# Four uneven zero transfers behind the last pass over wq, and twelve zero pieces sent as halves: a two-layer decode backward kernel on one core

## The chip, the core and the metric

The kernel runs on one core of one Trainium2 chip. The core has a matmul engine (PE, with its weight loads shown as PEld), a vector engine (DVE), a scalar engine (ACT), a general engine (POOL) and a queue engine (SP). Sixteen DMA engines move data between the chip's memory and the core's on-chip buffer (SBUF, 128 partitions). The metric is device time of one execution in microseconds, the median of several runs; less is better.

## The reference, cut to what matters

One token goes through two rounds of the same attention block A and the same MLP block B, and the kernel returns the output and all gradients.

```
def _fwd_reference(A_x, A_k_cache, A_v_cache, A_wq, A_wo, B_x, B_w1, B_b1, B_w2):
    x = A_x
    x = x + _A_ref(_layernorm(x), k_cache, v_cache, wq, wo)   # attention on the last 4096 of 32768 cache rows
    x = x + _B_ref(_layernorm(x), w1, b1, w2)                 # h * tanh(softplus(h)) MLP
    x = x + _A_ref(...)                                        # the same weights again
    x = x + _B_ref(...)
    return x
_out, _vjp = jax.vjp(_f, A_x, A_k_cache, A_v_cache, A_wq, A_wo, B_w1, B_b1, B_w2)
return (_out, *_vjp(grad_out))
```

Shapes: D = 1024, 32 query heads in 4 groups, head size 128, MLP width 3584, all bf16. The two cache gradients, `out_2` and `out_3`, are [1, 4, 32768, 128]. Attention reads only the last 4096 rows of each group, so the first 28,672 rows (ZR in the code) of each of the eight group planes are zero: 8 planes of 7 MB, 56 MB of zeros to be written. The rest of the outputs are weight gradients (outer products of two rows, one a round) and the small vectors.

## The kernel before, in words

The forward part streams the weights once or twice through a ring of eight 1 MB slots in SBUF (`ring_t`, class `Ring`; its loads are issued by SP at L71 as a slot comes free), then the backward part streams them again: for round 1 the pass over W1 that lies on the chip (`dn_b1`, L852), then `attn_bwd` (L905) with its pass over wo, the attention products against V and K, and its pass over wq; then round 0 in the same order (L1160 for w2, `dn_b0` L891, `attn_bwd` again). Chunks are transposed on PE, evicted by ACT or DVE, and used as the weights of matrix-vector products.

After the last pass over wq (the end of L1227) a late stage begins: all PSUM becomes four wide tiles, and `work` (L1140) takes turns among generators that make outer products (`unit_dw` L1072, `units_kv` L1122), evict them into 1 MB stages and hand them to SP to be stored (`store`, L1044, issued at L1050 and L1055, in halves or in wholes).

The zeros go beside all this from POOL's own queue. `zt` is a 128 x 4096 tile of zeros, filled by a memset at L811. `zjobs` (L246) is a list of 56 pieces: each of the 8 planes is cut into seven pieces of 128 partitions x 8 KB, 1 MB each. Half of one piece is written early, from another tile of zeros, by SP (L288); its other half, 0.5 MB, is put at the far end of the list (L291), so that it goes last of all. `zeros(n, after)` (L257) takes the next n pieces and issues one transfer for each (L265). With `after`, POOL first copies one element of that tile (L260), so that the transfers behind it on POOL's in-order queue wait for the tile. The number of pieces at each call is written out by hand:

- 1 and 7 around the forward attention of round 1, 8 after it (L841);
- 8 at L997, ahead of `dn_b1`, and 4 at L1001 behind it;
- 4 in `dp3` and 3 in `dq3` (around the round-1 attention products), 1 at L1154, 2 in the pass over w2, 2 at L1174;
- 2 in `do1` at c == 5, 4 in `dp1` and 4 in `dq1` (around the round-0 attention products), 2 in `dn1` at t == 3;
- 4 at L1228, behind the last pass over wq, the 0.5 MB piece last.

POOL also carries small copies: in `do1` at c == 1, `take_back` (L832) brings rows back from scratch memory as five transfers (28 pieces of 256 bytes into one partition, twice; then 2x32, 2x8 and 2x8 pieces into two partitions); at c == 5 and c == 6, `rows_go` (L1038, issued at L1041) moves 8 rows into one partition four times and 7 rows twice. SP's `twins` (L1066, issued at L1070) copy those rows once more for the outer products. In `attn_bwd`, POOL fills the second half of DOC (L927).

Of the kernel before, what the change touches and what calls it, by code (L numbers as in the profile page):

```python
# [15 lines left out]
P = 128  # L16
HQ = 32
DH = 128
# [3 lines left out]
G = 4  # L22
# [71 lines left out]
def kernel(  # L94
# [22 lines left out]
    nc = tc.nc  # L117
# [3 lines left out]
    ZR = Sk - W  # L121
# [9 lines left out]
    def sb(shape, dtype, name):  # L131
        return keep.tile(shape, dtype, name=name)
# [24 lines left out]
    ZC = 4096  # L157
    zt = sb([P, ZC], BF16, "zt")
# [36 lines left out]
    for hi in range(4):  # L195
        r = slice(32 * hi, 32 * hi + 32)
# [49 lines left out]
    zjobs = []  # L246
    for out_t in (out_2, out_3):
        for g in range(G):
            dst = out_t[0, g, 0:ZR, :].rearrange("(p r) d -> p (r d)", p=P).rearrange("p (r c) -> p r c", c=ZC)
            for k in range(dst.shape[1]):  # L250
                zjobs.append(dst[:, k, :])
    zjobs.reverse()

    pz = sb([1, 16], FP32, "pz")
    pz_n = [0]

    def zeros(n, after=None):  # L257

        if after is not None and zjobs:
            nc.gpsimd.tensor_copy(pz[0:1, pz_n[0] % 16:pz_n[0] % 16 + 1], after[0:1, 0:1])  # L260
            pz_n[0] += 1
        for _ in range(n):
            if zjobs:
                dst = zjobs.pop()
                nc.gpsimd.dma_start(dst, zt[:, 0:dst.shape[1]])  # L265


    KEEP_Q = (5, 6, 7)
# [96 lines left out]
    def to_eight(bank, buf):  # L365

        nc.vector.transpose(buf[:, 0:256], bank[:, 0:256])
        return buf[:, 0:256].rearrange("p (g m) -> p g m", m=32)[:, :, 0]
# [434 lines left out]
    def last_da(k):  # L803

        for c in (5, 6):
            if k == 0:
                da_dots(c)
            else:
                ring.release(("2", 0, c))
        if k:  # L810
            nc.gpsimd.memset(zt[:], 0.0)  # L811
            zeros(1)

    def wo_hook1(c):
        if c == 0:
            zeros(7, OC[:, 0, 1:2])
        if c:
            conv(1)
# [4 lines left out]
    def put_by(name, cols, n):  # L823

        b = big().bitcast(BF16)
        nc.tensor.transpose(b[0:2 * n, 0:P], cols[:].rearrange("p n l -> p (n l)"), ident_bf[:])
        r = stg[0:2 * n, len(DR), :]
        nc.scalar.copy(r, b[0:2 * n, 0:P])
        DR[name] = dram.tile([2 * n, P], BF16, name=f"dr_{name}")
        nc.sync.dma_start(DR[name][:], r)  # L830

    def take_back(name, base, off, step=2):  # L832
        r = DR[name][:].rearrange("(n l) p -> l n p", l=2)
        to = ROWS[base:base + 2, off:off + r.shape[1] * P].rearrange("l (n p) -> l n p", p=P)
        for l in range(0, 2, step):
            nc.gpsimd.dma_start(to[l:l + step], r[l:l + step])

    x3, st3, sA1 = attn_fwd(1, x2, st2, False, wo_hook1, last_da)
    put_by("OC", OC, HQ)
    put_by("NA", NA, TD)  # L840
    zeros(8, x3)  # L841
    sB1 = mlp_fwd(1, x3, st3, lambda: conv(1, "A"))
    put_by("NB", NB, TD)
# [4 lines left out]
    dh1, dh0 = mp1, mp0  # L848
# [3 lines left out]
    def dn_b1(g):  # L852

        bcast(lambda c: DHC[:, c, 1:2], STAY)
        mv_open()
        even()
        for t in range(TD):
            rowdot(W1[:, t, 0:STAY * P], [LB[0][:, 0:512]], 512, dnp[:, t:t + 1], True)
            for k in range(3):
                f0, n = STAY + 8 * k, 8  # L860
                w = W1[:, t, f0 * P:(f0 + n) * P]
                turned(w, n, lambda w=w, f0=f0, n=n, t=t, k=k: mv(w, n, TP[:, t:t + 1], lambda i: DHC[:, f0 + i, 1:2], k == 2),
                       None, f_block)
        flush()
        conv(3, "A")
        return ln_bwd(dnp, sB1["n32"], sB1["rstd"], g, "B1", lambda k: conv(k, "A"))
# [3 lines left out]
    def rowize_f():  # L870

        b = big().bitcast(BF16)
        for l in range(2):
            for k in range(4):
                nc.tensor.transpose(b[0:7, (4 * l + k) * P:(4 * l + k + 1) * P],
                                    DHC[:, :, l].rearrange("p (c k) -> p k c", k=4)[:, k], ident_bf[:])
        nc.scalar.copy(rf.rearrange("c (l p k) -> c l p k", l=2, k=4), b[0:7].rearrange("c (l k p) -> c l p k", l=2, k=4))
        for l in range(2):
            rows_out.append((ROWS[64 + l:65 + l, NOFF:NOFF + F].rearrange("o (c j) -> o c j", j=512),
                             rf[:, 512 * l:512 * l + 512]))  # L880
# [113 lines left out]

    nc.vector.tensor_tensor(out=dh1[:], in0=da1[:, 0:TF], in1=mp1[:], op=ALU.mult)
    nc.vector.tensor_copy(DHC[:, :, 1], dh1[:])
    zeros(8, dh1)  # L997
    g3 = dn_b1(g4)
    sB1["act_late"]()
    put_by("AC", AC, TF)  # L1000
    zeros(4, g3)  # L1001

    def dp3():
        zeros(4)
# [22 lines left out]
    def rowize(cols, n, base, off):  # L1027

        b = big().bitcast(BF16)
        nc.tensor.transpose(b[0:2 * n, 0:P], cols[:].rearrange("p n l -> p (n l)"), ident_bf[:])  # L1030
        k = rt_n[0]
        rt_n[0] += 1
        nc.scalar.copy(rt[0:2 * n, k, :], b[0:2 * n, 0:P])
        for l in range(2):
            rows_out.append((ROWS[base + l:base + l + 1, off:off + n * P].rearrange("o (t p) -> o t p", p=P),
                             rt[l:2 * n:2, k, :]))

    def rows_go(queue):  # L1038

        while rows_out:  # L1040
            queue.dma_start(*rows_out.pop(0))  # L1041
# [24 lines left out]
    def twins(*of):  # L1066
        for base, n in of:
            for l in range(2):
                to, of = (base ^ 32) + l, base + l
                nc.sync.dma_start(*(x.rearrange("l (a b) -> l a b", a=16) for x in (TWIN[to:to + 1, 0:n], ROWS[of:of + 1, 0:n])))  # L1070
# [116 lines left out]
    def do1(c):  # L1187
        if c == 1:
            take_back("AC", 96, NOFF, 1)
            take_back("OC", 32, NOFF)  # L1190
            take_back("NB", 64, 0)
            take_back("NA", 0, 0)
        if c == 4:
            y = to_eight(YR, RT.rearrange("p a t s -> p (a t s)")[:, 0:512].bitcast(FP32))
            nc.vector.tensor_tensor(out=x4[:], in0=y, in1=x3[:], op=ALU.add)
        if c == 5:
            rowize(GA, TD, 32, 0)
            rowize(GB, TD, 96, 0)
            rows_go(nc.gpsimd)
            zeros(2)  # L1200
        if c == 6:
            rowize_f()
            rows_go(nc.gpsimd)

    def dp1():
        zeros(4)
        twins((96, NOFF + F), (32, NOFF + J), (64, NOFF + F))
        stage_free.extendleft(VS[:, g].rearrange("p t d -> p (t d)") for g in range(G))

# [7 lines left out]
    def dn1(t):  # L1217
# [6 lines left out]
        if t == 5:  # L1224
            todo[0].append(units_cols(0, 8, out_4))

    g0_rest = attn_bwd(0, sA0, g1, ("o", 3), ("q", 3), (), dict(do=do1, dp=dp1, dq=dq1, dn=dn1))  # L1227
    zeros(4)  # L1228
    stage_free.extendleft(ring_t[:, i, :] for i in range(8))
    stage_free.extendleft(lent)  # L1230

# [50 lines left out]
```

## Time and profile before

| What | us |
|---|---|
| median of 3 runs (lowest, highest) | 450.59 (450.19, 450.88) |
| the profiled execution | 450.31 |
| its span, first to last instruction | 448.5 |
| PE busy | 314.8 (70%) |
| DVE busy | 262.2 (58%) |
| ACT busy | 209.4 (47%) |
| POOL busy | 44.5 (10%) |
| bytes moved by the DMA engines | 181.40 MB, mean 404 GB/s |
| share of POOL's queue (software_dynamic) | 58.26 MB, 31.5% of the 16 engines' span |
| zero transfers, issue to landing, median | 20.7 |

The profile is one execution taken by the hardware profiler. Its page cuts the span into 40 slices of 11.2 us and shows each engine's busy share as a digit. For the DMA engines it gives the mean share of all 16, and what they moved. The windows view gives the same for any stretch of time, and a share can come out a little over 1, since packets overlap at their ends. A wait names who ended it. The trace also has a record for every DMA packet (queue, start, duration, size, but not which of the 16 engines carried it) and the time of every completion step: a transfer completes in 16 steps, one from each DMA engine.

### The profile page before, as it was taken

What the parts mean: (1) busy time and instruction counts of PE and PEld (TensorE: products, weight loads), DVE (VectorE), ACT (ScalarE), POOL (GpSimd) and SP (SyncE); (2) the same over time, 40 slices, a digit from 0 to 9 for tenths busy, and PEclk for the clock granted to TensorE, in tenths of its full rate; (3) what the DMA queues carried; (4) which work ended last, traced back from release to release, by engine and by line L of the source; (5) the groups of instructions that cost most, each with busy time, mean ns of one, the idle gap of its engine ahead of it and who ended that gap; (6) DMA issues with size and microseconds to landing.
All of it is one profiled execution on the core that took longest, in us unless ns stands there. A gap on an engine that the chain in (4) does not pass through costs nothing.

```text
span 448.5 us, 12849 instructions
## 1 busy us (share of the span) xinstructions
PE 314.8 (70%) x5681; PEld 243.3 (54%) x5681; DVE 262.2 (58%) x516; ACT 209.4 (47%) x238; POOL 44.5 (10%) x94
## 2 busy tenths in 40 slices
PE   3835542565698797987987666798877888899600
PEld 3735532445685696986986545798862222234300
DVE  4504746368551664864477447654478998998600
ACT  2501101011058576861474341561348999999700
POOL 1000000001232212102101003023220000000000
PEclk9955555556559799986799657957685555555555
DMA  8999999999999999999999999999999899999994
GB/s 336 422 420 420 419 419 418 418 355 425 400 422 421 422 422 416 397 422 422 424 422 422 427 423 419 405 410 388 405 397 412 347 411 416 416 420 411 409 406 192
DMA packets 30057, 181.40 MB, mean 404 GB/s; under 512 B 3954, under 2 KB 5162, under 8 KB 12082
## 3 DMA queue, kind: packets, MB, share of 16 engines
q1 hardware_dynamic: 21478, 122.30, 66.6%
q0 software_dynamic: 8432, 58.26, 31.5%
q8 instruction: 44, 0.72, 0.6%
q14 instruction: 11, 0.09, 0.0%
q10 hardware_dynamic: 92, 0.02, 0.0%
HBM read 81.84 MB, written 98.62 MB: 402 GB/s over the span
## 4 chain that ended last, share of the span: by engine, by line
DMA 40%; PE 31%; DVE 13%; ACT 5%; issue 4%; SPq 0%; ACTq 0%; DVEq 0%
DMA ring<-in_B_w_dram 13%; PE BIG L489 10%; DMA W<-in_A_wo_dram 9%; DMA ring<-in_A_wq_dram 7%; DMA ring<-in_A_wo_dram 5%; DMA W<-in_B_w_dram 4%; PE TP L508 4%; PE wide L1129 4%; ACT ring L316 3%; PE wide L1078 3%; DVE ring L313 3%; DMA W<-in_A_k_cache_dram 2%; DVE W L313 2%; PE BIG L667 2%; PE MV L956 2%
## 5 line engine op out<-in xcount | busy, mean ns | idle before, releaser
L316 ACT COPY ring<-BIG 128x1024 bf16<-128x1024 bf16 x52 | 51.4, 1014 | 50.0 <-PE BIG L489 30.2
L1078 PE MATMUL wide<-W 2*128 2x512 bf16 x240 | 53.1, 597 | 9.7 <-ACT ring L316 2.4
L489 PE MATMUL BIG<-ident_bf,ring 128*128 128x128 bf16 x672 | 54.5, 234 | 2.0 <-issue 1.2
L489 PEld LDWEIGHTS <-ring 128*128 128x128 bf16 x768 | 51.6, 107 | 3.4 <-issue 2.7
L466 DVE CUSTOM_DVE_ANT_0 junk<-ring,SC 128x1024 bf16<-128x1024 bf16 x32 | 38.9, 1215 | 11.0 <-DMA ring<-in_B_w_dram 10.6
L1078 PEld LDWEIGHTS <-W 2*128 2x128 bf16 x240 | 12.8, 102 | 46.3 <-issue 45.4
L508 PEld LDWEIGHTS <-ring 128*128 128x128 bf16 x864 | 29.9, 98 | 11.7 <-issue 6.3
L316 ACT CAST ring<-wide 128x1024 bf16<-128x1024 f32 (+1 forms) x37 | 34.5, 1015 | 1.1 <-PE wide L1078 1.1
L265 POOL DMA_DIRECT2D out_dram<-zt x56 | 29.9, 538 | 48.8 <-DMA out_dram<-zt 47.9
L313 DVE CAST ring<-wide 128x1024 bf16<-128x1024 f32 (+1 forms) x27 | 31.3, 1198 | 2.8 <-PE wide L1078 2.7
L316 ACT COPY KT<-BIG 128x1024 bf16<-128x1024 bf16 x22 | 21.6, 1007 | 21.8 <-PE BIG L667 19.9
L313 DVE COPY ring<-BIG 128x1024 bf16<-128x1024 bf16 x32 | 21.8, 689 | 15.1 <-PE BIG L489 12.5
L466 DVE CUSTOM_DVE_ANT_0 junk<-ring,DSX 128x1024 bf16<-128x1024 bf16 x24 | 29.4, 1224 | 0.8
L489 PE MATMUL BIG<-ident_bf,W 128*128 128x128 bf16 x280 | 26.9, 255 | 3.1 <-DMA W<-in_A_wo_dram 2.7
L316 ACT COPY W<-BIG 128x1024 bf16<-128x1024 bf16 x20 | 20.1, 1014 | 11.8 <-PE BIG L489 11.6
L551 PE MATMUL MV<-NA,ring 128*128 128x1 bf16 x512 | 15.3, 165 | 13.4 <-DMA ring<-in_A_wq_dram 12.1
L489 PEld LDWEIGHTS <-W 128*128 128x128 bf16 x288 | 21.6, 123 | 3.5 <-DMA W<-in_A_wo_dram 2.9
L551 PEld LDWEIGHTS <-ring 128*128 128x128 bf16 x512 | 14.7, 104 | 14.2 <-DMA ring<-in_A_wq_dram 12.8
L1129 PE MATMUL wide<-W 32*128 32x256 bf16 x128 | 19.7, 403 | 1.5 <-DVE KT L313 0.9
L316 ACT CAST KT<-wide 128x1024 bf16<-128x1024 f32 x19 | 19.1, 1030 | 1.6 <-PE wide L1129 1.1
L316 ACT CAST W<-wide 128x1024 bf16<-128x1024 f32 x16 | 16.0, 1024 | 6.6 <-PE wide L1078 6.2
L354 PE MATMUL YR<-ring,AC 128*32 128x256 bf16 x208 | 10.9, 367 | 11.1 <-DMA ring<-in_B_w_dram 8.7
(279 smaller groups left out, 524.5 us busy)
## 6 DMA issues: line engine op xcount, KB each, us to landing
out_dram<-zt POOLq DMA_DIRECT2D x55, 1024.0 KB, 20.7
ring<-in_A_wq_dram SPq DMA_DIRECT2D x24, 1024.0 KB, 12.8
ring<-in_A_wo_dram SPq DMA_DIRECT2D x14, 1024.0 KB, 19.0
ring<-in_B_w_dram SPq DMA_DIRECT2D x13, 1024.0 KB, 18.9
W<-in_A_wo_dram SPq DMA_DIRECT2D x10, 1024.0 KB, 19.9
out_dram<-ring SPq DMA_DIRECT2D x15, 512.0 KB, 11.1
W<-in_B_w_dram SPq DMA_DIRECT2D x8, 896.0 KB, 18.4
out_dram<-ring SPq DMA_DIRECT2D x5, 1024.0 KB, 12.3
```

Source lines behind the costliest of these rows:

```text
L265: nc.gpsimd.dma_start(dst, zt[:, 0:dst.shape[1]])
L313: nc.vector.tensor_copy(dst, src)
L316: nc.scalar.copy(dst, src)
L354: nc.tensor.matmul(bank[32 * j:32 * j + 32, 0:n].rearrange("p (g a) -> p g a", a=m.shape[-1]), lhsT=vec.to_broadcast([P, 32]), rhs=m, star ...
L466: nc.vector.tensor_tensor_reduce(out=out, in0=a, in1=vec, scale=1.0, scalar=acc if i else 0.0, op0=ALU.mult, op1=ALU.add, accum_out=acc)
L489: nc.tensor.transpose(b[:, i * P:(i + 1) * P], block(w, i) if block else w[:, i * P:(i + 1) * P], ident_bf[:])
L508: nc.tensor.matmul(out, lhsT=w[:, i * P:(i + 1) * P], rhs=rhs_of(i), start=fresh[0], stop=last and i == n - 1, skip_group_check=True)
L551: nc.tensor.matmul(q_ps[:, h:h + 1], lhsT=ch[:, h * P:(h + 1) * P], rhs=NA[:, t, l:l + 1], start=(k == 0 and h == 0), stop=(k == TD - 1), ...
L667: nc.tensor.transpose(b[:, i * P:(i + 1) * P], T[:, g, 8 * b8 + i, :], ident_bf[:])
L956: nc.tensor.matmul(dq_ps[:, g_ * 8:g_ * 8 + 8], lhsT=KT[:, g_, t, :], rhs=DSX[:, c:c + 8], start=(g_ == 0 and t == 0), stop=(t == TS - 1), ...
L1078: nc.tensor.matmul(b[:, 512 * i:512 * i + 512], lhsT=R[at:at + 2, lo:lo + P], rhs=R[at:at + 2, ro + 512 * i:ro + 512 * i + 512], start=Tru ...
L1129: nc.tensor.matmul(b[:, k * 256:(k + 1) * 256], lhsT=RT[32 * g:32 * g + 32, a, tp, :], rhs=YS[32 * g:32 * g + 32, :], start=True, stop=Tru ...
```

## The change

The plane of group 3 of `out_3`, the last in the list, is cut differently: its 896 units of 8 KB (4096 bf16 elements) are split into 512 units, `zless`, and three ordinary 1 MB pieces. The list then has 52 entries. The four pieces at L1228 are replaced by `zeros_less()`, which writes the 512 units in four transfers: from 4 partitions of `zt` (0, 4, 8, 12) 33 units each, from partition 16 17 units, from 3 partitions (20, 24, 28) 33 each, and from 8 partitions (64, 68, ..., 92) 33 each. The 0.5 MB piece is now the last entry of the list and so goes in `dn1`'s call.

`zeros` gets a third argument, `parts`. With 2, each piece goes as two transfers of half its columns (128 x 4 KB). This is used for the last 2 of the 8 pieces at L997, the 4 at L1001, the 2 in `do1` and the 4 in `dp1`: twelve pieces, 24 transfers. All other calls stay, and so does the total of zeros written.

```
-            dst = out_t[0, g, 0:ZR, :].rearrange("(p r) d -> p (r d)", p=P).rearrange("p (r c) -> p r c", c=ZC)
-            for k in range(dst.shape[1]):
-                zjobs.append(dst[:, k, :])
+            rest = out_t[0, g, 0:ZR, :]
+            if (out_t, g) != (out_3, G - 1):
+                dst = rest.rearrange("(p r) d -> p (r d)", p=P).rearrange("p (r c) -> p r c", c=ZC)
+            else:
+                units = rest.rearrange("(u r) d -> u (r d)", r=ZC // DH)
+                zless, dst = units[0:4 * P], units[4 * P:].rearrange("(r p) c -> p r c", p=P)
+            zjobs += [dst[:, k, :] for k in range(dst.shape[1])]
...
-    def zeros(n, after=None):
+    def zeros(n, after=None, parts=1):
...
-                nc.gpsimd.dma_start(dst, zt[:, 0:dst.shape[1]])
+                m = dst.shape[1] // parts
+                for k in range(parts):
+                    nc.gpsimd.dma_start(dst[:, k * m:(k + 1) * m], zt[:, 0:m])
+
+    def zeros_less():
+        at = 0
+        for k, p, n in ((4, 0, 33), (1, 16, 17), (3, 20, 33), (8, 64, 33)):
+            nc.gpsimd.dma_start(zless[at:at + k * n].rearrange("(k n) c -> k n c", k=k),
+                                zt[p:p + 4 * k:4, None, :].to_broadcast([k, n, ZC]))
+            at += k * n
...
-    zeros(8, dh1)
+    zeros(6, dh1)
+    zeros(2, None, 2)
...
-    zeros(4, g3)
+    zeros(4, g3, 2)
...
-            zeros(2)
+            zeros(2, None, 2)
...
-        zeros(4)
+        zeros(4, None, 2)
         twins((96, NOFF + F), (32, NOFF + J), (64, NOFF + F))
...
     g0_rest = attn_bwd(0, sA0, g1, ("o", 3), ("q", 3), (), dict(do=do1, dp=dp1, dq=dq1, dn=dn1))
-    zeros(4)
+    zeros_less()
```

## The prediction

> **What bounds the kernel.** I read the 40 slices first, for the engine that has no slack.
>
> ```profile
> DMA  8999999999999999999999999999999899999994
> GB/s 336 422 420 420 419 419 418 418 355 425 400 422 421 422 422 416 397 422 422 424 422 422 427 423 419 405 410 388 405 397 412 347 411 416 416 420 411 409 406 192
> ...
> HBM read 81.84 MB, written 98.62 MB: 402 GB/s over the span
> ```
>
> The reader is to see the DMA row: nine tenths or more in 37 of 40 slices, at 405 to 425 GB/s. The exceptions are the start, slice 31 (349 to 360 us) and the last slice, 192 GB/s. The kernel is bound by transfers, and only what fills a hole or moves the last byte forward can pay. So I asked for the holes by windows (columns: us; busy PE, PEld, DVE, ACT, POOL; clock; DMA share; GB/s).
>
> ```profile
> 344.00:348.00 4.00, 2.96 (x19) 0.85 (x20) 2.55 (x3) 3.36 (x5) 0.00 (x0) 0.50 1.02 406
> 351.00:354.00 3.00, 2.39 (x13) 0.66 (x11) 3.00 (x4) 2.79 (x5) 0.00 (x0) 0.50 0.87 341
> 354.00:356.00 2.00, 1.40 (x10) 0.35 (x8) 2.00 (x3) 2.00 (x4) 0.00 (x0) 0.50 0.73 291
> 356.00:360.00 4.00, 3.61 (x17) 0.84 (x16) 3.67 (x5) 4.00 (x5) 0.00 (x0) 0.50 0.87 345
> 420.00:438.00 18.00, 2.21 (x16) 1.15 (x13) 2.28 (x2) 3.45 (x4) 0.00 (x0) 0.50 1.02 408
> 438.00:441.50 3.50, 0.00 (x0) 0.00 (x0) 0.00 (x0) 0.00 (x0) 0.00 (x0) 0.50 1.02 407
> 441.50:443.50 2.00, 0.00 (x0) 0.00 (x0) 0.00 (x0) 0.00 (x0) 0.00 (x0) 0.50 0.44 172
> 443.50:447.00 3.50, 0.00 (x0) 0.00 (x0) 0.00 (x0) 0.00 (x0) 0.00 (x0) 0.50 0.07 27
> ```
>
> From 438 us on nothing computes; queued stores drain. From 443.5 to 447 the share is 0.07, which is 1.1 of 16 DMA engines: one engine works alone on its part of the stores while fifteen are done. The packet records give the ends: most engines' last packet between 442.1 and 442.8, one at 443.06, one at 443.41, the last at 447.16 us. I call that last one the straggler.
>
> How old is its lag? Each transfer completes in 16 steps, one an engine. For every store from 355.9 to 441 us the last step comes 5.0 to 5.9 us behind the median one, and for the zero transfers issued between 306 and 328 us 5.9 to 6.8 us. So it is not built up in the last stage but carried into it, together with this: the zeros issued at 331.6 land at 345.6 on the median engine and at 355.5 on the straggler. Whatever zero bytes it is spared before 356 us come off its end.
>
> **The change, part by part.** *The four uneven transfers.* Out go the last four zero transfers (3.5 MB: three of 1 MB and one of 0.5 MB); the 0.5 MB piece moves up into the last call of the pass, so 0.5 MB moves back and 4 MB, 512 units of 8 KB, stand behind the pass. They go as four transfers over 4, 1, 3 and 8 source partitions: fifteen partitions of 33 units and one of 17. Even, each engine had 32. An 8 KB packet takes 0.316 us of an engine at 414 GB/s (8192 B over 414/16). If each partition is one engine's work and the 17 units are the straggler's, it has 15 units less, 4.74 us, and the others one more, 0.32 us. The straggler then ends at 447.16 - 4.74 = 442.42, and the last of the others at 443.41 + 0.32 = 443.73, which sets the end: 447.16 - 443.73 = 3.43 us gained. What is late next is that second engine.
>
> What these transfers cost in issue: POOL spent 533 ns on a transfer of 128 pieces, 703 ns on the one of 32x2 and 597 ns on one of 8x2, so (703-597)/48 = 2.2 ns a piece in the two-row form; 512 pieces on top of four starts of 0.56 us (the 8x2 ones' 563) are about 3.4 us against 4 x 0.533 = 2.1. POOL has nothing behind them, and the queue still holds zeros issued at 314.7 to 328.5, which land until 335.3. Nothing.
>
> *The twelve halves.* The same bytes in 24 transfers: 12 more issues.
>
> ```profile
> L265 POOL DMA_DIRECT2D out_dram<-zt x56 | 29.9, 538 | 48.8 <-DMA out_dram<-zt 47.9
> ```
>
> Among the waits (total us, times, longest):
>
> ```profile
> POOL out_dram L265 <- DMA out_dram<-zt: 47.9, 22, 4.7
> ```
>
> 12 x 0.533 = 6.4 us more of POOL, which is 10% busy: hidden. The second line, from the list of waits, shows the other price: zeros wait for zeros. From 143 to 189 us each issue comes only when the transfer eight before it has landed, so eight are in flight; with halves this is 4.2 MB instead of 8.4, 10.1 us of transfer at 414 GB/s. Behind a waiting issue on POOL stand a copy of DOC (L927; the half that it fills is read only after the pass), the rows that feed the weight products (L1041), and further zeros. The two transfers of L1041 at 303.2 would wait for the eighth before them, now the first rows of L1041, landed at 304.1: 0.9 us later, and SP's copies of those rows (L1070) and the weight products after 333 us have room for it. Where the eight halves run dry: straggler's lag up to 6.8 us, plus 4.2 us from issue to first landing (306.81 to 310.97), against 10.1 us: up to 0.9 us of idle on the other engines around 310, which does not touch the straggler, but would touch the end once it is relieved.
>
> What halves can win: where zeros and loads share an engine, packets alternate (8 KB of zeros, 8 KB of load, 187 to 267 us, each about 200 GB/s). With 4 KB zeros a load gets two thirds instead of half. That helps the wq loads at 183 to 218 us, but the chain of work has PE and ACT there, no load; the chain's loads (in_B_w at 229 to 265, in_A_wo at 276 to 294 us) run beside pieces that stay whole. Zeros that give way come back later, the bytes being the same. The most it can win is what stands empty later, the windows 351 to 360 against a share of 1.02: 3 x 0.15 + 2 x 0.29 + 4 x 0.15 = 1.6 us. I take nothing, being nearest to where the chain has no load, and keep -1.6 and +0.9 for the range.
>
> **The sum.** The profiled execution took 450.31 us with a span of 448.5, and 1.8 around it. 450.31 - 3.43 = 446.9; the median of the runs shown, 450.59, lies 0.28 higher: 447.2.
>
> **Which engine gets the 17?** This is the open step; the trace names no engines, but the small POOL transfers mark them. The 28-, 8- and 7-row copies into one partition each used the same 14, 8 and 7 engines every time (back-to-back packets of one copy and the next on the same engine), and the straggler is among the seven. The three copies of 2x32 and 2x8 pieces used three different pairs, one after the other, and the straggler is in the third pair. So counted in the order in which pairs were dealt, it is the fifth or the sixth. If the uneven transfers are dealt from the same start, or by groups of four source partitions (the 17 come from partition 16, the fifth group), the fifth gets the 17. If the dealing goes on behind the third pair, the 17 fall on the eleventh.
>
> [...]
>
> **Rivals.** *The 17 miss the straggler*: it gets 33 like the rest, one unit more than now, +0.32: 450.9. For it: dealing that goes on. Against: by the other two readings it is hit half the time or more.
>
> *The 17 pieces do not go to one engine*: like the 28-row copy, two to an engine, they spread over nine, and one engine is left out by the other three. If that one is the straggler (the sixth, where dealing goes on), it loses 30 units, the others gain up to 3 (0.95 us): end at 443.41 + 0.95 = 444.36, 447.8. If not, the straggler gains 3 units: 451.5.
>
> *Two shares on one engine, slower*: if each transfer starts over at the same engine, as the 8- and 7-row copies did, shares pile up. One doubled share puts 66 units on an engine that had 32: 34 x 0.316 = 10.7 us, end 442.4 + 10.7 = 453.1 against 447.16: 456.5. All four on the first: 116 units, 26.5 us, 472. It decides as soon as an engine has over 15 units too many (4.74 us). Against: the pairs did not pile up.
>
> **How the numbers follow.** Hit on one engine 0.55; spread with the straggler left out 0.05; miss 0.22; spread with the straggler loaded 0.05; piled up 0.13. Faster by over 0.2% (0.9 us, about what a measurement here can tell from no change): 0.60. Within: 0.22. Slower: 0.18. The likeliest case's own range is 447.2 - 1.6 to 447.2 + 0.9, or 445.6 to 448.1; the miss with its +0.9 and the loaded straggler reach 451.8. Piling up is left out: 445.4 to 451.8.
>
> **What would show it.** Right: the last window of 3.5 us with a share of 0.07 is gone, the share falls from 1.02 to 0 within some 1.5 us, and zeros in the last of the four transfers land without a step 9.9 us late. Miss: the lone engine is still there for 4 us. Piling up: it is there for over 10 us, at 0.06 or 0.13. Halves wrong: load waits between 183 and 265 us move by more than a microsecond, or windows around 310 us lose their share of 1. The prediction fails if the straggler is made anew by something after 356 us, or if freed room lets the next engine fall behind.

## The result, and the profile after

The changed kernel takes **456.54 us** (455.87 to 456.84), the one before beside it 450.50 (450.19 to 450.88): a ratio of 1.0125, 95% interval 1.0108 to 1.0141. The forecast was 447.2, with a range of 445.4 to 451.8. It is 6.0 us slower, where 3.4 us of gain were expected. Ratios leave out slow runs, those more than 1.5% above the fastest of the same kernel, which concerns own_swap below alone: its ratio rests on its runs of 454.9 and 457.09 us, its median on all four.

In the new file the zero transfers are issued at L271 and the uneven ones at L278. The 40 slices of the kernel after (11.4 us each, the span being 454.9):

```profile
DMA  8999999999999999999999999998999999999994
GB/s 336 421 419 418 420 420 419 417 364 416 397 422 421 422 420 416 396 420 422 419 420 424 424 422 398 403 415 335 392 345 371 323 405 415 420 421 410 408 407 189
...
HBM read 81.84 MB, written 98.62 MB: 397 GB/s over the span
```

The bytes are the same. The DMA row is at nine tenths nearly everywhere, as before, but the second row falls to 335 GB/s in the 28th slice (307 to 318 us, where the share is lower too) and to 345, 371 and 323 GB/s in the 30th to 32nd (330 to 364 us), where the share is not. The second dip has to be looked at by windows (columns as in the prediction: us; busy PE, PEld, DVE, ACT, POOL; clock; DMA share; GB/s). The kernel after:

```profile
344.00:348.00 4.00, 2.66 (x12) 0.58 (x12) 2.76 (x4) 4.00 (x5) 0.00 (x0) 0.50 1.01 379
351.00:354.00 3.00, 2.29 (x16) 0.67 (x14) 3.00 (x4) 2.80 (x5) 0.00 (x0) 0.50 1.01 314
354.00:356.00 2.00, 1.63 (x10) 0.39 (x10) 2.00 (x2) 2.00 (x3) 0.00 (x0) 0.50 0.99 330
356.00:360.00 4.00, 3.69 (x19) 1.22 (x17) 3.63 (x4) 4.00 (x6) 0.00 (x0) 0.50 0.89 306
420.00:438.00 18.00, 1.14 (x7) 0.51 (x4) 1.21 (x2) 2.56 (x3) 0.00 (x0) 0.50 1.02 408
438.00:441.50 3.50, 0.00 (x0) 0.00 (x0) 0.00 (x0) 0.00 (x0) 0.00 (x0) 0.50 1.02 407
441.50:443.50 2.00, 0.00 (x0) 0.00 (x0) 0.00 (x0) 0.00 (x0) 0.00 (x0) 0.50 1.02 408
443.50:447.00 3.50, 0.00 (x0) 0.00 (x0) 0.00 (x0) 0.00 (x0) 0.00 (x0) 0.50 1.02 408
447.00:450.00 3.00, 0.00 (x0) 0.00 (x0) 0.00 (x0) 0.00 (x0) 0.00 (x0) 0.50 0.48 193
450.00:453.50 3.50, 0.00 (x0) 0.00 (x0) 0.00 (x0) 0.00 (x0) 0.00 (x0) 0.50 0.10 40
```

Two things are to be seen. **First**, from 351 to 354 us the share is 1.01 and the rate 314 GB/s; before, the share was 0.87 and the rate 341. Before, some engines were idle there; now all are busy and move less. So each packet takes longer. The packet records say it directly: the 8 KB zero packets that start between 334 and 352 us last 361 ns on average, 14% of them over 400; before it was 316 ns, with 1%. **Second**, the lone engine at the end is still there: its window with a share of 0.07 (443.5 to 447 before) is now the one from 450 to 453.5, with 0.10. Taking the last store alone, the median engine finishes it at 442.62 us before and at 448.50 after, and the straggler 4.9 and 5.4 us behind that. The whole queue ends 6 us later, tail included.

A ledger over the windows' rates gives the place. Up to 436 us the kernel before moved 178.69 MB, the one after 176.13. Of the 2.56 MB that are missing, 0.46 are lost between 190 and 306 us, 0.55 from 306 to 318, 1.41 from 330 to 362, and 0.16 from 362 to 378. At 412 GB/s that is 6.2 us, about the 5.9 that the median engine moved. Not each of these amounts need be the change's: less_only and own_even below, which are the same program up to the uneven transfers, differ by 0.70 MB between 190 and 306 us and by 0.70 MB the other way between 306 and 330. So the 0.46 MB may be a shift of that kind; the 1.41 MB are twice as much.

The page's group of ordinary zeros, of the kernel after:

```profile
L271 POOL DMA_DIRECT2D out_dram<-zt x64 | 34.2, 536 | 80.3 <-DMA out_dram<-zt 79.6
```

And two lines of its waits (total us, times, longest):

```profile
POOL out_dram L271 <- DMA out_dram<-zt: 79.6, 37, 4.6
POOL out_dram L278 <- DMA out_dram<-zt: 4.8, 3, 2.1
```

Zeros wait 79.6 us for zeros instead of 47.9, and the uneven transfers wait too. That is the price of eight in flight that the prediction had named (the issue at 145.61 us starts 0.28 us after the last step of the transfer eight before it); whether it costs time is for the experiments. The order of the compute instructions on each engine is unchanged.

### The profile page after: what moved, and what is told of

The parts are those of the page before. It is cut to its first block, busy times and chain, and to the rows that moved or that the text cites. A ratio compares the mean times of both kernels' runs of the same rounds, so it can differ in the third digit from the quotient of the medians.

```text
span 454.9 us, 12861 instructions
## 1 busy us (share of the span) xinstructions
PE 311.8 (69%) x5681; PEld 239.8 (53%) x5681; DVE 261.7 (58%) x516; ACT 209.3 (46%) x238; POOL 51.4 (11%) x106
## 5 line engine op out<-in xcount | busy, mean ns | idle before, releaser
L504 PE MATMUL BIG<-ident_bf,ring 128*128 128x128 bf16 x672 | 53.4, 232 | 0.7 <-issue 0.3
L504 PEld LDWEIGHTS <-ring 128*128 128x128 bf16 x768 | 50.7, 106 | 1.9 <-issue 1.2
L271 POOL DMA_DIRECT2D out_dram<-zt x64 | 34.2, 536 | 80.3 <-DMA out_dram<-zt 79.6
L523 PEld LDWEIGHTS <-ring 128*128 128x128 bf16 x864 | 29.6, 97 | 13.9 <-issue 7.6
L504 PE MATMUL BIG<-ident_bf,W 128*128 128x128 bf16 x280 | 22.8, 229 | 3.1 <-DMA W<-in_A_wo_dram 2.4
L566 PEld LDWEIGHTS <-ring 128*128 128x128 bf16 x512 | 14.5, 103 | 13.8 <-DMA ring<-in_A_wq_dram 12.4
L504 PEld LDWEIGHTS <-W 128*128 128x128 bf16 x288 | 18.3, 111 | 3.9 <-DMA W<-in_A_wo_dram 3.1
```

The source lines that it names most:

```text
L271: nc.gpsimd.dma_start(dst[:, k * m:(k + 1) * m], zt[:, 0:m])
L504: nc.tensor.transpose(b[:, i * P:(i + 1) * P], block(w, i) if block else w[:, i * P:(i + 1) * P], ident_bf[:])
L523: nc.tensor.matmul(out, lhsT=w[:, i * P:(i + 1) * P], rhs=rhs_of(i), start=fresh[0], stop=last and i == n - 1, skip_group_check=True)
L566: nc.tensor.matmul(q_ps[:, h:h + 1], lhsT=ch[:, h * P:(h + 1) * P], rhs=NA[:, t, l:l + 1], start=(k == 0 and h == 0), stop=(k == TD - 1), ...
```

## Experiments

Three theories at first. *Foreign partitions*: a transfer from few source partitions makes packets longer, whatever the shares are. *Halves run dry*: the 0.55 MB and more that are lost before 330 us set the end. *Doubled share*: the prediction's third rival, two shares of the units on one engine. Each ratio is against the kernel before, run beside it on the same chip (450.46, 450.55 or 450.53 us). Where a diff shows only the tuple, the loop of `zeros_less` is as in the change and all other pieces go whole.

**The halves alone** (halves_only): the list and the last four pieces as before.

```
-    zeros_less()
+    zeros(4)
```

> The twelve halves alone; the last four pieces go as before. If the halves cost what the empty stretch of the after profile around 306 to 318 us shows (335 GB/s against 388, about 0.6 MB, 1.4 us): 451.5 to 452.5 us. If they carry the whole loss (the queue of zeros runs dry): 455.5 to 457. If only the uneven transfers cost: 450 to 451.

451.03 us (450.64 to 451.26), ratio 1.0011 [1.0002, 1.0021]. Two windows of the kernel before:

```profile
306.00:318.00 12.00, 10.23 (x281) 9.53 (x281) 4.29 (x11) 0.26 (x1) 4.63 (x10) 0.59 0.97 386
352.00:360.00 8.00, 6.60 (x34) 1.65 (x30) 7.67 (x8) 7.79 (x10) 0.00 (x0) 0.50 0.81 322
```

The same two of the halves alone:

```profile
306.00:318.00 12.00, 11.35 (x292) 10.86 (x291) 4.28 (x11) 0.83 (x2) 5.27 (x12) 0.50 0.88 340
352.00:360.00 8.00, 7.00 (x39) 2.27 (x37) 7.04 (x7) 7.82 (x9) 0.00 (x0) 0.50 1.03 407
```

The queue does run dry around 310 us, at 340 GB/s against 386: 0.55 MB, 1.3 us. But the zeros that are late fill the hole at 352 to 360 us, 407 GB/s against 322, so nearly all of it is given back. The halves are not the cause. They have a second price that does not need an empty queue: the median 4 KB zero packet lasts 159 ns, the median 8 KB one 309 (140 to 330 us). Two of the one are 9 ns longer than one of the other, and with 96 such pairs on each engine that makes 0.9 us (my estimate).

**The uneven transfers alone** (less_only): the change's list and tuple, all pieces whole.

```
-    zeros(4)
+    zeros_less()
```

> The four uneven transfers alone, all other pieces whole. If reading each share from one partition makes the packets longer (404 against 315 ns at 338 to 340 us): 454.5 to 456, with 310 to 380 GB/s from 336 to 356 us and the straggler still there. If a share landed twice on one engine: the same time, but with packets of 315 ns and one engine working alone for over 8 us at the end. If only the halves cost: 450.5 to 451.

458.34 us (456.84 to 458.81), ratio 1.0171 [1.015, 1.0192], 2.3 us over the range expected for longer packets. The uneven transfers make the loss by themselves. The kernel before:

```profile
336.00:344.00 8.00, 5.86 (x27) 1.66 (x24) 7.70 (x12) 7.26 (x9) 0.00 (x0) 0.50 1.00 413
344.00:352.00 8.00, 6.62 (x32) 1.68 (x33) 6.38 (x6) 7.36 (x9) 0.00 (x0) 0.50 1.02 407
```

The uneven transfers alone:

```profile
336.00:344.00 8.00, 6.04 (x26) 1.75 (x25) 7.84 (x10) 7.78 (x10) 0.00 (x0) 0.50 0.96 338
344.00:352.00 8.00, 5.51 (x29) 1.41 (x30) 5.41 (x8) 6.03 (x8) 0.00 (x0) 0.50 1.00 348
352.00:360.00 8.00, 6.39 (x33) 1.50 (x28) 7.67 (x7) 7.79 (x10) 0.00 (x0) 0.50 0.75 261
```

Up to 352 us the engines are busy at 338 to 348 GB/s where the kernel before moved 413 and 407. Zero packets there last 373 ns on average.

**The same with even shares** (less_even): sixteen partitions of 32 units, four at a time.

```
-        for k, p, n in ((4, 0, 33), (1, 16, 17), (3, 20, 33), (8, 64, 33)):
+        for k, p, n in ((4, 0, 32), (4, 16, 32), (4, 64, 32), (4, 80, 32)):
```

> As less_only, but the 512 units as four transfers of 4 partitions with 32 units each: the same few-engine form without the small share. If the form costs (packets longer on all engines): as less_only, within 0.7 us. If the loss came from where the 17 units went: 450 to 451.

462.72 us (457.85 to 463.88), ratio 1.0254 [1.0198, 1.031]; packets 364 ns. Every partition gives the same number of units and it is still slower, so the uneven share is not the cause. A common first engine for all four transfers, which would put the 512 units on four engines, is excluded too: fourteen engines have finished the last of the four by 355.0 us, the others at 362.5 and 379.9. It is 4.4 us over less_only, where 0.7 were expected, but its four times lie far apart; I read no more than the sign from it.

**One transfer over sixteen partitions** (one16): every eighth partition, 32 units each.

```
+        nc.gpsimd.dma_start(zless.rearrange("(k n) c -> k n c", k=16),
+                            zt[0:P:8, None, :].to_broadcast([16, 32, ZC]))
```

> The 512 units as one transfer over 16 partitions, 8 apart, 32 units each: one partition an engine, but all sixteen engines at once and evenly. If reading 32 units from a single partition is what makes packets long: as less_only. If it is the dealing of a few engines at a time: 450 to 451.

463.76 us (460.61 to 465.74), ratio 1.0312 [1.0269, 1.0355]. That is 5.4 us over less_only, which neither expected case had, and it is the clearest record of the cause:

```profile
336.00:344.00 8.00, 5.19 (x26) 1.61 (x25) 6.44 (x11) 5.27 (x8) 0.00 (x0) 0.50 0.98 208
344.00:352.00 8.00, 4.96 (x21) 1.15 (x21) 4.97 (x6) 6.70 (x8) 0.00 (x0) 0.50 0.96 234
```

A share of 0.98 and half the rate, 208 GB/s: the median zero packet from 336 to 352 us lasts 635 ns, twice the usual 309. The 4 KB packets of the stores get longer too, 238 ns on average against 161 in own_even below. The engines are as busy as in the kernel before (1.00, at 413 GB/s) and move half, so I looked at which partitions they read, and took up the prediction's reading by groups of four for the next theory: *groups*. The change's sixteen partitions (0, 4, ..., 28 and 64, ..., 92), each with its three neighbours, are sixteen groups, one for each engine in the order of dealing; an engine also reads its group in the ordinary transfers and in the stores; packets get longer when another engine reads that group; and the few-partition transfers are dealt to consecutive engines, not beginning at the first but going on behind the three two-row copies, for which the trace of before shows three different pairs, that is, at the seventh. In the change the seventh engine would then read partition 0, which is the first engine's, and so on. All of this is assumed: no trace names an engine or the partitions that it reads. The next runs test what follows from it.

**The cut of the list alone** (whole4): the 512 units as four ordinary transfers.

```
+        for q in range(4):
+            nc.gpsimd.dma_start(zless[q * P:(q + 1) * P], zt[:])
```

> The list cut as in the change, all pieces whole, and the 512 units as four ordinary transfers of 128 partitions: the control for less_only. Every theory: 450 to 451, as before, since only the place of one half piece differs.

450.42 us (450.2 to 451.03), ratio 0.9994 [0.9984, 1.0005]; packets 313 ns. The destinations and the 0.5 MB that moved up cost nothing.

**Each engine its own group, even shares** (own_even): by the theory, two partitions for the seventh and eighth engine, eight for the ninth to sixteenth, six for the first to sixth.

```
+        for k, p, n in ((2, 24, 32), (8, 64, 32), (6, 0, 32)):
```

> The 512 units from 2, 8 and 6 partitions (24 and 28; 64 to 92; 0 to 20), 32 units each. Theory: dealing goes on behind the third small pair, so the three transfers fall on engines 7 to 8, 9 to 16 and 1 to 6, and each engine reads the partitions that it also reads in ordinary transfers; packets stay near 315 to 330 ns: 450 to 452. Rival, the few-partition form costs wherever it is put: 457 to 463 as less_even. Rival, dealing starts over at the first engine: pairs of engines read the same partitions as stores of others, 457 to 463.

450.61 us (449.79 to 451.28), ratio 1.000 [0.9991, 1.001]; packets 313 ns.

**The same dealing, other sources** (own_swap): only the source partitions of the first and third transfer differ; counts and destinations stay, and so do the engines if the dealing does not look at the source.

```
+        for k, p, n in ((2, 0, 32), (8, 64, 32), (6, 8, 32)):
```

> own_even with the same three transfers over the same engines and 32 units each; only the source partitions differ: 0 and 4 in place of 24 and 28, and 8 to 28 in place of 0 to 20, so eight engines read another engine's group and eight their own. If the reading of a foreign group beside its owner is the cost: packets over 330 ns on average and 454 to 461 us. If only the form or the dealing costs: as own_even, 450 to 451.5.

459.45 us (454.9 to 462.62), ratio 1.0123 [1.0094, 1.0152]. Own_even's windows first:

```profile
336.00:344.00 8.00, 5.69 (x27) 1.74 (x27) 6.44 (x11) 6.63 (x10) 0.00 (x0) 0.50 1.01 420
344.00:352.00 8.00, 6.93 (x33) 1.80 (x31) 7.64 (x8) 7.79 (x10) 0.00 (x0) 0.50 1.02 402
352.00:360.00 8.00, 7.00 (x41) 2.20 (x37) 6.94 (x7) 7.72 (x10) 0.00 (x0) 0.50 1.03 410
```

And own_swap's, whose profiled execution is the 454.9:

```profile
336.00:344.00 8.00, 6.03 (x26) 1.75 (x25) 7.81 (x11) 7.66 (x10) 0.00 (x0) 0.50 0.98 383
344.00:352.00 8.00, 6.08 (x29) 1.50 (x30) 5.93 (x7) 6.63 (x9) 0.00 (x0) 0.50 1.01 382
352.00:360.00 8.00, 6.42 (x31) 1.71 (x31) 7.68 (x8) 7.80 (x10) 0.00 (x0) 0.50 0.52 194
```

This pair isolates the cause: both read the same sixteen partitions (0 to 28 and 64 to 92, every fourth), 32 units from each, and write the same places; only which transfer reads which partition differs, and with it, by the theory, which engine. In own_swap the loss falls in two places: 382 GB/s at a full share up to 352 us, and then a share of 0.52. There half the engines, on average, have run out while the others still hold work.

**Dealing that starts over** (two8): two transfers of eight. Begun at the first engine, the partitions would, by the theory, be each engine's own.

```
+        for k, p, n in ((8, 0, 32), (8, 64, 32)):
```

> The 512 units from 8 partitions (0 to 28) and 8 partitions (64 to 92), 32 units each, sixteen groups of four partitions, one for each engine. If dealing goes on behind the third pair, each engine reads the group of an engine six places before it, beside that engine's stores: packets of 350 ns and more, 456 to 463. If dealing starts at the first engine, or follows the partition: 450 to 452.

461.14 us (457.18 to 463.06), ratio 1.0227 [1.0168, 1.0287]; packets 354 ns. So, if the theory holds, dealing does not start over; it goes on, as own_even assumed.

**Own groups, and 18 units for the fifth and the sixth engine** (own_less): the change's idea, aimed by the dealing that own_even assumed.

```
+        for k, p, n in ((2, 24, 34), (8, 64, 34), (4, 0, 34), (2, 16, 18)):
```

> As own_even, but the fifth and the sixth engine, one of which should be the straggler, get 18 units and the others 34. Theory: the straggler loses 14 units (4.4 us), the others gain 2 (0.6 us), the end falls from 447.2 to 444 us of the profile: 447 to 448.5. If the straggler is neither of the two: 451 to 452.5. If the form costs: 455 to 462.

**447.04 us** (446.61 to 447.8), ratio 0.9928 [0.9905, 0.9952]: faster than both kernels. The end of its profile:

```profile
441.00:444.00 3.00, 0.00 (x0) 0.00 (x0) 0.00 (x0) 0.00 (x0) 0.00 (x0) 0.50 0.21 85
444.00:447.00 3.00, 0.00 (x0) 0.00 (x0) 0.00 (x0) 0.00 (x0) 0.00 (x0) 0.50 0.00 0
```

The lone engine's window is gone. The last store's four late steps come 2.0 to 2.9 us behind the median engine (441.31); in own_even the last one came 6.4 behind.

**Relieve only the sixth** (own_out6): the fifth keeps a full share. Two units are left over and go from partitions 0 and 1 (by the same dealing, on the sixth and the seventh engine).

```
+        for k, p, n in ((2, 24, 34), (8, 64, 34), (5, 0, 34)):
...
+        nc.gpsimd.dma_start(zless[at:], zt[0:2, :])
```

> Own partitions; the sixth engine gets nothing of the 512 units, the fifteen others 34 (two of them 35). If the straggler is the sixth: it loses 32 units, the others set the end, 447 to 448.5. If it is the fifth: it gains 2 units, 0.6 us, 451 to 452.

451.39 us (451.08 to 452.64), ratio 1.0025 [1.0016, 1.0035]. The tail of 6.3 us stays:

```profile
444.00:447.00 3.00, 0.00 (x0) 0.00 (x0) 0.00 (x0) 0.00 (x0) 0.00 (x0) 0.50 0.08 33
```

By that dealing the straggler is the fifth engine: sparing the fifth and the sixth took 3.5 us off (own_less), sparing the sixth alone took off none (own_out6).

**The whole change with own_less's tuple** (own_less_halves): own_less with all twelve halves.

```
-    zeros(2, None, 1)
+    zeros(2, None, 2)
...
-    zeros(4, g3, 1)
+    zeros(4, g3, 2)
...
-            zeros(2, None, 1)
+            zeros(2, None, 2)
...
-        zeros(4, None, 1)
+        zeros(4, None, 2)
```

> The whole change, halves included, with the uneven transfers drawn from each engine's own partitions as in own_less. If the halves alone cost half a microsecond (as in halves_only): 447.3 to 448. If they help once the straggler is relieved: under 446.8. If both interfere as in the change, where halves made less_only 1.8 us better: 445 to 446.

449.05 us (448.38 to 449.73), ratio 0.9966 [0.9955, 0.9977]. I had expected the halves to cost about as little as alone; they cost 2.0 us.

```profile
441.00:444.00 3.00, 0.00 (x0) 0.00 (x0) 0.00 (x0) 0.00 (x0) 0.00 (x0) 0.50 1.02 408
444.00:447.00 3.00, 0.00 (x0) 0.00 (x0) 0.00 (x0) 0.00 (x0) 0.00 (x0) 0.50 0.40 163
```

Here the share stays full to 444 us: the engines finish within 3.5 us of one another, the median one 4.2 us later than in own_less. The queue does not run dry around 310 us this time. Own_less:

```profile
306.00:318.00 12.00, 9.83 (x242) 9.15 (x239) 3.90 (x8) 0.53 (x2) 3.36 (x8) 0.52 1.01 420
```

Own_less_halves:

```profile
306.00:318.00 12.00, 9.52 (x275) 8.96 (x273) 3.59 (x10) 0.26 (x1) 4.67 (x10) 0.50 1.00 403
```

The engines are busy and move less, in line with the longer time of two 4 KB packets. By the same ledger own_less_halves is 1.57 MB behind own_less at 436 us, 0.81 of it lost between 190 and 306. Alone, the halves had lost 0.81 MB between 190 and 330 (0.23 of it before 306) and won 0.70 back between 330 and 362, where the kernel before has its hole. Own_less has no hole there (405 GB/s against 387), so nothing can be won back. That and the 0.9 us of the packets fit the difference, but neither was tried by itself, and why the loss before 306 us is larger here is open.

## Why the prediction was wrong, point by point

**What bounds the kernel: right.** Transfers do, and one engine's lag sets the end. Sparing that engine 14 units, with the sources placed as in own_even, gained 3.5 us (own_less). By the prediction's own sum, with two units more on the others, it would be 447.16 - (443.41 + 2 x 0.316) = 3.1 us.

**A unit's price, 0.316 us: the step that failed.** The prediction took the 512 units for work of that size whatever partitions they come from, and asked only to which engine they go. The price depends on which transfer reads which partitions. In the change it was 361 ns on average from 334 to 352 us. In the same window it was 313 ns a packet in own_even, whole4 and own_less, 334 to 373 ns in own_swap, two8, less_even, less_only and the change, and 574 ns in one16. The stores beside them pay as well: their 4 KB packets last 183 ns on average in the change and 238 in one16 (336 to 352 us), against 163 before and 161 in own_even. Which engines carry the longer store packets, the trace does not tell. The row that stood for it in the trace of before was the ordinary 128-partition transfer, and such a transfer does not show it. I gave no bounds on this term.

What the runs show of the cause is this: 208 GB/s in one16 where own_even moves 420, and 450.61 against 459.45 us in the pair own_even and own_swap, which read the same sixteen partitions. That an engine pays when another reads the same group agrees with the times of own_even, own_swap, two8, less_even and less_only, but it stays my reading of them; on one16, which reads partitions outside the sixteen groups too, it says nothing.

**Which engine gets the 17: wrong, and the open step was rightly called open.** That the straggler is the fifth or the sixth in the order of dealing was right, if the dealing is as own_even assumed. But, by the count of small packets, no engine gets the 17. The page's line of the kernel before:

```profile
DMA packets 30057, 181.40 MB, mean 404 GB/s; under 512 B 3954, under 2 KB 5162, under 8 KB 12082
```

The same line of the kernel after:

```profile
DMA packets 32889, 181.41 MB, mean 399 GB/s; under 512 B 5250, under 2 KB 6458, under 8 KB 16450
```

And of own_less:

```profile
DMA packets 31465, 181.41 MB, mean 407 GB/s; under 512 B 5362, under 2 KB 6570, under 8 KB 13490
```

The counts come out if an engine that has no part in a transfer of k partitions gets one 4-byte packet for each unit of a partition. Own_less: 14 engines x 34, 8 x 34, 12 x 34 and 14 x 18 make 1408, and 3954 + 1408 = 5362, to the packet. In the change there are 1296 more than before; twelve more transfers of 16 completion packets are 192, which leaves 1104. (One16 has three transfers fewer than the kernel before and 3906 of these packets, 3 x 16 less than 3954; less_only, with as many transfers as before, has 5058, 1104 more.) The transfers over 4, 3 and 8 partitions make 12 x 33 + 13 x 33 + 8 x 33 = 1089. The 17 units then have 15: not 15 x 17 = 255, as on one engine, but what comes of nine engines with two units each, the last with one (7 x 2 + 1). So the counts speak for the second rival, the spread over nine. If it did not move the dealing on, which no run shows by itself, the other three transfers went from the seventh engine round to the fifth and left out the sixth, and the straggler, the fifth, had 33 units and two more. For that case the prediction gave 451.5, at 0.05. I put the 5.0 us from there to 456.5 down to the longer packets; no run separates them from the halves.

**Two shares on one engine: it gave 456.5, and was not it.** The number agrees by chance. Its sign was a lone engine for over 10 us; the lone stretch at the end is some 5 us as before, and the median engine is 5.9 us late. Own_even excludes it: if each transfer began at the same engine, two engines would have 96 of the 512 units each, and it is at 1.000. The packet counts cannot decide this, for they are the same wherever a transfer begins.

**Issue of the uneven transfers, nothing: right.** Four at L278 with 4.8 us of waits, and own_even, issued in the same way, is at 1.000.

**The halves, nothing with bounds -1.6 and +0.9: right alone** (+0.5, from a loss of 1.3 us around 310 us that is given back at 352 to 360), and right in where they run dry. The 0.9 us of the smaller packets were not in the sum; the prediction took the same bytes for the same time. **Too narrow in company**: 2.0 us in own_less_halves. In the change itself they seem to help, 456.54 against less_only's 458.34, but the two profiled executions (456.64 us and, the fastest of its four, 456.84) have spans of 454.9 and 455.0 and bytes up to 436 us within 0.1 MB, so the traces show no place for these 1.8 us. That stays open.

**Three smaller points.** Of the 37 slices that the prediction puts at 405 to 425 GB/s, six lie outside, from 355 to 427; the ninth (90 to 101 us) has 355 GB/s at nine tenths, so a fall in the rate at a full share stood in the profile of before, with a cause that stays open. The slice that the prediction puts at 349 to 360 us is the one from 347.6 to 358.8. And the lower end of the range, 445.4, is 0.2 below the 445.6 that its terms give.

**What else stays open**: why it is the fifth engine that falls behind. Own_less and own_out6 show, by the dealing assumed, which one it is, not the reason. In the kernel before, the last completion step of the zeros falls further and further behind the median one from 139 us (1.1 us) to 187 us (6.6).

## What to carry to other kernels

A DMA from a few source partitions is not a free way to choose an engine: with the same sixteen source partitions, own_even took 450.61 us and own_swap 459.45. The sign here was a full DMA share with a fallen rate and packets longer than their size asks for (one16: 0.98, 208 GB/s, 635 ns for 8 KB against 309). If an engine is to be relieved, find with even shares a placement of the sources that costs nothing (own_even, 1.000) before making the shares unequal (own_less, 0.9928). A price taken from a row is known only for the access pattern of that row (here 316 ns a unit before, 361 in the change).

## What the runs showed of the hardware

- **Source partitions**: with units read from every eighth partition, 0 to 120, the rate was halved (one16: median zero packet 635 ns against 309, 208 GB/s at a share of 0.98 against own_even's 420 at 1.01 in the same window). The same sixteen partitions, read by other transfers: 450.61 against 459.45 us (own_even, own_swap). That engines have groups of their own is my reading; no trace names an engine.
- **Dealing**: with the same even shares, 450.61 us in own_even and 461.14 in two8. If the groups are as assumed, dealing went on from one transfer to the next for these transfers over two and more partitions, and its start at the seventh engine fits only if the 28-, 8- and 7-row copies into one partition left it where it was.
- **A late finish in the change**: four engines finish the uneven transfer over three partitions at 357.6 to 360.3 us, 5.6 to 5.8 us after the one ahead of it (352.0 to 354.5). I take these for the four that carry the first transfer and get 33 small packets of the third, but no run isolates it. Such packets need not cost time: by the same count own_even has 1024, and is at 1.000.
- **Half-size zero transfers**: with eight in flight (an issue of halves at 189 to 229 us starts 0.28 to 0.29 us after the last step of the transfer eight before it), half the bytes wait in the queue. From 306 to 318 us two executions with halves fell to 340 GB/s at shares of 0.87 and 0.88 (the change, halves_only; before 386 at 0.97); in own_less_halves the share stayed at 1.00, at 403 GB/s. A 4 KB zero packet takes 159 ns, an 8 KB one 309 (medians).
